# Feature matmuls on two halves of the array's rows, 65-column products on two halves of its columns

## The chip, the cores and the metric

One core of a Trainium2 chip runs the program. The metric is device time in microseconds (us). The kernel before takes 995.03 us, the median of three runs (994.74 to 995.92).

## The reference

Three layers run one after the other. The first is an attention without a softmax over the keys; the other two are feed-forward layers on 2304 tokens.

```python
# q, k, v: (4, 8, 576, 64) = batch, head, token, d;  omega: (128, 64)
def phi(x):                                   # x is scaled by 64 ** -0.25 first
    proj = einsum('bhsd,md->bhsm', x, omega)  # 128 features of each token
    h = proj - sum(x * x, -1, keepdims=True) / 2
    return exp(h - max(h, -1, keepdims=True)) / sqrt(128)
kv  = einsum('bhsm,bhsd->bhmd', phi(k), v)
z   = sum(phi(k), axis=2)
out = einsum('bhsm,bhmd->bhsd', phi(q), kv) / (einsum('bhsm,bhm->bhs', phi(q), z) + 1e-6)

x = out as (2304, 512)                        # d_ff 2048, then 1536
x = relu(x @ w_in) ** 2 @ w_out
x = rmsnorm(x) * g;  x = (silu(x @ w_gate) * (x @ w_val)) @ w_out2
```

Outside the kernel only the layout is changed. A column of ones stands beside v, so that one product of 65 columns gives both the numerator and the denominator.

## The kernel before, in words

Work goes by blocks: four of 512 tokens, one for each batch, and a remainder of 256 tokens (64 of each batch). Attention handles a batch as four pairs of heads. The 512 tokens of a pair are four tiles of 128 (`R` is 4), and the 64 left-over tokens of q and of k form one more tile for each pair, the remainder.

For one pair the PE does this. **Features** (L595 to L604): the transposed q or k of two heads stands as 128 rows (64 of d for one head, 64 for the other) by 512 tokens. Each tile of 128 tokens is the stationary operand, and the moving operand `bd` is block-diagonal, 128 rows by 256 columns, with omega for one head in the upper left and for the other in the lower right. So one matmul of depth 128 and 256 columns gives the features of both heads, and half of the products are with zeros. In batches 0 and 1 (`FULL` is 2) it is one plain fp32 matmul. In batches 2 and 3 operands are split into a high and a low part of type fp32r, and three fp32r matmuls stand for it; the split of each operand is a CAST on ACT and a subtraction on DVE or POOL (`operand`, L550). There are 36 tiles of features in a batch: four pairs by four of k, four of q and one of the remainder. **kv** (L671, L674): five matmuls of 65 columns for each head, four tiles and the remainder. **The output rows** (L731): four matmuls of 65 columns for each head. That makes 18 products of 65 columns in a pair and 72 in a batch, all plain fp32 with a stationary operand of 128 columns. Between them stand transposes through the array (L658, L726, L763, L773) and two 65-column products for the left-over queries (L735), whose stationary operand has 64 columns. A plain fp32 matmul stands in the trace as two records, each with its weight load.

DVE takes a maximum over each bank of features (L615) and two small operations (L619), and ACT the exponentials (L628). Further on the first feed-forward layer (`moe1`) has its hidden products at L845 and its output products at L875, all fp32r; the second layer has L1082 and L1143.

All instructions are nodes of a planner (`Plan`), which simulates the engines with the cost written beside each node and emits the nodes in the order in which its simulation starts them. Buffers come from classes with a fixed number of slots. PSUM has two banks of class `t`, two of `h`, four of `acc`. After batch 0 attention may use the two `t` banks alone. Until its own clock reaches 45 us, the planner also puts fillers on the PE where it finds nothing ready there: two fp32r matmuls of 256 columns on a constant (L484 to L487). An engine runs its instructions in the emitted order. All DMAs are issued from SP, in one order.

Attention of batch b+1 is planned beside `moe1` of batch b, and the weights of the second layer are brought into another form and stored to DRAM during the first.

Of the kernel before, what the change touches and what calls it, by code (L numbers as in the profile page):

```python
# [247 lines left out]
def kernel(  # L248
# [23 lines left out]
    nc = tc.nc  # L272
# [12 lines left out]
    FULL = 2  # L285
# [3 lines left out]
    EPS_DEN = 1e-6 * M  # L289

# [38 lines left out]
    plan.alloc["tr"] = slot_alloc("att", "tr", [P, 4, P], F32R)  # L329
    plan.alloc["tt"] = slot_alloc("att", "tt", [P, 4, P], F32R)  # L330
    plan.alloc["p"] = slot_alloc("att", "p", [P, 2 * R, M], F32)
    plan.alloc["pr"] = slot_alloc("att", "pr", [P, 2, M], F32)
# [16 lines left out]
    bd = const.tile([P, 2, M], F32, name="bd")  # L349
    bd_hi = const.tile([P, 2, M], F32R, name="bd_hi")  # L350
    bd_lo = const.tile([P, 2, M], F32R, name="bd_lo")
# [9 lines left out]
    b_bd, b_bds = Buf(ap=bd), Buf(ap=bd_hi)  # L361
# [14 lines left out]
    def dve(n):  # L376
        return 0.07 + n * 0.00104
# [87 lines left out]
    def emit_zero():  # L465
        nc.gpsimd.memset(bd, 0.0)

# [12 lines left out]
    plan.add("POOL", 0.5, T0, emit_zero, w=[b_bd])  # L480
# [14 lines left out]
    def emit_bd():  # L495
        for h in range(2):
            ps = slice(h * D, (h + 1) * D)
            nc.scalar.activation(out=bd[ps, h, :], in_=om2[ps, :], func=AF.Copy, scale=SCALE)

    def flat(t):  # L500
        return t.rearrange("p h m -> p (h m)")

    plan.add("ACT", 0.5, T0, emit_bd, [b_om, b_bd], [b_bd])
    split(T0 + (60 if FULL else 1), lambda: flat(bd), lambda: flat(bd_hi), lambda: flat(bd_lo), 256, [b_bd],
          (b_bds, 0), (b_bds, 1))

# [28 lines left out]
    def attention(b):  # L535
# [3 lines left out]
        full, long = b < FULL, b >= LONG  # L539
        rem_x = []  # L540
# [9 lines left out]
        def operand(prio, ldp, src, cls):  # L550

            if full:
                x = Buf(["lt", cls], view=lambda t: t if len(t.shape) == 2 else t.bitcast(F32).rearrange("p a n -> p (a n)"))
                dma(ldp, lambda: x.ap, src, 262144, w=[x])
                return x,
            x, th, tl = Buf(["lt"]), Buf([cls]), Buf([cls])
            dma(ldp, lambda: x.ap, src, 262144, w=[x])
            split(prio, lambda: x.ap, lambda: th.ap.rearrange("p a n -> p (a n)"),
                  lambda: tl.ap.rearrange("p a n -> p (a n)"), 512, [x], th, tl, "ANY")
            return th, tl  # L560
# [759 lines left out]
```

## Time and profile before

| | |
|---|---|
| median of three runs | 995.03 us |
| span of the profiled execution | 994.4 us |
| PE busy | 980.4 us, 99% |
| DVE, ACT, POOL busy | 72%, 53%, 10% |
| granted TensorE clock, mean | 1.000 |
| DMA, mean | 180 GB/s |

The page gives for the profiled execution its span, from the first to the last instruction; the median of the runs is 0.6 us above it, and this is taken as what lies around the span. A row of the timeline gives the start of a group of equal instructions, its length and its count. The end of a matmul is modelled and overlaps the next one, so the price of a record is read from the start of a group to the start of the next, divided by the count.

### The profile page before, as it was taken

Reading aid. Unit: us, or ns where it says so; the run is one execution under the profiler, and the core shown is the slowest. Engines: PE = TensorE matmul, PEld = TensorE weight load, DVE = VectorE, ACT = ScalarE, POOL = GpSimd, SP = SyncE. Lnnn points to the kernel's source line nnn. Section 1 sums busy time; section 2 is a strip of 40 time slices with the busy share of each in tenths; the row PEclk is TensorE's granted clock in tenths of the full one; section 3 lists DMA queues with packets and bytes.
Section 4 is the critical chain, followed back from the end, with each engine's and each line's share of the span. In section 5 each row is a group of like instructions: output and inputs, shape, how many; then the busy total and the mean of one; then the engine's idle time right before and its main releaser. Section 6 shows DMA issues by size and latency. Waiting matters only on the chain.

```text
span 994.4 us, 14580 instructions
## 1 busy us (share of the span) xinstructions
PE 980.4 (99%) x5130; PEld 832.7 (84%) x5130; DVE 712.0 (72%) x1393; ACT 523.7 (53%) x1093; POOL 100.5 (10%) x86
## 2 busy tenths in 40 slices
PE   8999999999999999999999999999999999999998
PEld 7878888888888888888789978888887888888887
DVE  6988998777658576665532989889798747576673
ACT  6988877665465455545444657664353444314220
POOL 2222222221110101000000101000000000000000
PEclk9999999999999999999999999999999999999999
DMA  8777888876667565778768534334234221212213
GB/s 270 240 245 259 278 287 292 300 267 214 248 217 257 189 248 188 237 247 285 273 222 273 169 107 150 93 117 127 77 116 136 75 64 53 74 43 75 65 32 105
DMA packets 74840, 179.35 MB, mean 180 GB/s; under 512 B 8848, under 2 KB 12048, under 8 KB 74768
## 3 DMA queue, kind: packets, MB, share of 16 engines
q1 hardware_dynamic: 74768, 178.43, 54.7%
q8 instruction: 40, 0.66, 0.3%
q14 instruction: 32, 0.26, 0.1%
HBM read 143.27 MB, written 35.13 MB: 179 GB/s over the span
## 4 chain that ended last, share of the span: by engine, by line
PE 86%; DVE 7%; DMA 3%; issue 1%; ACT 1%; SPq 0%; POOL 0%; ACTq 0%; DVEq 0%; POOLq 0%
PE acc L875 18%; PE h L845 18%; PE acc L1082 11%; PE t L1143 10%; PE h L1082 10%; PE t L1082 3%; PE t L731 3%; PE t L604 3%; PE t L671 2%; PE t L601 2%; DMA st<-y 2%; PE t L726 1%; DVE cc L1102 1%; PE h L1143 1%; DVE oa L1151 1%
## 5 line engine op out<-in xcount | busy, mean ns | idle before, releaser
L875 PE MATMUL acc<-g,wr 128*128 128x512 f32 (+1 forms) x660 | 151.9, 373 | 1.4 <-POOL g L394 1.2
L845 PE MATMUL h<-x,wr 128*128 128x512 f32 x528 | 133.9, 396 | 0.0
L875 PEld LDWEIGHTS acc<-g,wr 128*128 128x128 f32 x660 | 113.5, 189 | 21.5 <-POOL g L394 1.4
L1143 PE MATMUL t<-wq,ub 128*128 128x512 f32 x474 | 116.8, 391 | 1.5 <-DVE oa L1151 1.4
L403 ACT CAST wq<-wq 128x512 fp32r<-128x512 f32 x108 | 66.3, 619 | 98.1 <-DMA wq<-w2d3g 17.7
L845 PEld LDWEIGHTS h<-x,wr 128*128 128x128 f32 x528 | 97.2, 188 | 19.2
L1143 PEld LDWEIGHTS t<-wq,ub 128*128 128x128 f32 x474 | 88.4, 188 | 22.5 <-DVE oa L1151 2.9
L1082 PE MATMUL acc<-x,wq 128*128 128x512 f32 x324 | 106.9, 389 | 0.0
L394 DVE TENSOR_TENSOR wq<-wq 128x512 fp32r<-128x512 f32 x108 | 77.5, 726 | 29.5 <-ACT wq L403 29.2
L394 DVE TENSOR_TENSOR g<-f,g 128x512 fp32r<-128x512 f32 (+1 forms) x68 | 49.6, 729 | 65.9 <-ACT f L515 55.4
L859 ACT ACTIVATE f<-h 128x512 f32<-128x512 f32 (+1 forms) x80 | 45.1, 564 | 90.0 <-PE h L845 87.2
L1082 PE MATMUL h<-x,wq 128*128 128x512 f32 x252 | 85.3, 390 | 0.0
L1082 PEld LDWEIGHTS acc<-x,wq 128*128 128x128 f32 x324 | 60.8, 188 | 12.7
L875 PE MATMUL acc<-g,wu 128*128 128x512 f32 (+1 forms) x300 | 70.1, 375 | 1.2 <-DVE g L394 1.2
L1082 PE MATMUL acc<-xa,wq 128*128 128x512 f32 x192 | 69.8, 389 | 0.0
L628 ACT ACTIVATE p<-t,sm 128x128 f32<-128x128 f32 x212 | 59.2, 388 | 17.6 <-DVE sm L619 17.6
L1102 DVE TENSOR_TENSOR cc<-acc,cc 128x512 f32<-128x512 f32 x84 | 57.7, 687 | 13.6 <-PE acc L1082 11.8
L1151 DVE TENSOR_TENSOR oa<-t,oa 128x512 f32<-128x512 f32 x75 | 50.9, 687 | 21.8 <-PE t L1143 21.3
L845 PE MATMUL h<-x,wu 128*128 128x512 f32 x240 | 60.6, 395 | 0.0
L1082 PE MATMUL h<-xa,wq 128*128 128x512 f32 x168 | 60.5, 389 | 0.0
L875 PEld LDWEIGHTS acc<-g,wu 128*128 128x128 f32 x300 | 51.5, 189 | 10.5 <-DVE g L394 1.8
L441 ACT ACTIVATE dw<-st 128x512 f32<-128x512 f32 x67 | 45.6, 691 | 19.9 <-DMA st<-in_w_out_dram 8.1
(252 smaller groups left out, 1802.1 us busy)
## 6 DMA issues: line engine op xcount, KB each, us to landing
wr<-w1d SPq DMA_DIRECT2D x88, 512.0 KB, 4.3
st<-in_w_out_dram SPq DMA_DIRECT2D x28, 512.0 KB, 4.6
w1d<-wr SPq DMA_DIRECT2D x22, 512.0 KB, 4.6
st<-in_w_in_dram SPq DMA_DIRECT2D x16, 512.0 KB, 4.5
st<-in_w_gate_dram SPq DMA_DIRECT2D x12, 512.0 KB, 5.6
st<-in_w_val_dram SPq DMA_DIRECT2D x12, 512.0 KB, 5.4
st<-y SPq DMA_DIRECT2D x23, 256.0 KB, 4.2
v<-in_v_r_dram SPq DMA_DIRECT2D x16, 260.0 KB, 3.4
```

The source lines that it names most:

```text
L394: return lambda: en.tensor_tensor(out=lo(), in0=src(), in1=f32(hi()), op=ALU.subtract)
L403: first = plan.add("ACT", act(n), prio, lambda: nc.scalar.copy(out=hi(), in_=src()), rd, [whi], after, pre=[blo] if blo is not bhi else [])
L441: lambda: nc.scalar.activation(out=out(), in_=hf(), func=AF.Abs, scale=65536.0), [(st, 1)], [w])
L604: nc.tensor.matmul(o, lhsT=xs[x].ap[:, cidx, :], rhs=flat(w), start=n == 0, stop=n == 2)
L628: nc.scalar.activation(out=pbuf.ap[:, j0 + i, :], in_=fp.ap[:, i, :], func=AF.Exp, bias=mx.ap[:, i:i + 1])
L845: nc.tensor.matmul(hb.ap[:, :n], lhsT=u.ap[:, wl, kk * P:(kk + 1) * P], rhs=xcols(j, xl, kk)(), start=(gi == 0 and ii == 0), stop=(gi == l ...
L859: lambda: nc.scalar.activation(out=rb.ap[:, :n], in_=hb.ap[:, :n], func=AF.Relu), [hb], [rb])
L875: nc.tensor.matmul(accs[e].ap[:, :n], lhsT=u.ap[:, w, es], rhs=x.ap[:, :n], start=(c == 0 and i == 0), stop=(c == C1 - 1 and i == 2))
L1082: nc.tensor.matmul(bank.ap[:, cols], lhsT=u.ap[:, wl, c0 + kk * P:c0 + (kk + 1) * P], rhs=x[kk][xl].ap[:, :cols.stop - cols.start], start= ...
L1102: lambda: nc.vector.tensor_tensor(out=out.ap, in0=bank.ap, in1=x.ap, op=ALU.add), [bank, x], [out])
L1143: nc.tensor.matmul(o.ap, lhsT=x[xl].ap[:, c0:c0 + P], rhs=us[f"o{i}"].ap[:, wl, :], start=i == n == 0, stop=i == 1 and n == 2)
L1151: lambda: nc.vector.tensor_tensor(out=oa.ap, in0=o.ap, in1=oa.ap, op=ALU.add), [o, oa], [oa])
```

## The change

The block-diagonal operand goes. Its place takes `oms`, omega scaled, once on rows 0 to 63 and once on rows 64 to 127. Each tile of features becomes two plain fp32 matmuls of depth 64 and 128 columns: one head on the upper half of the array's rows, the other on the lower half, each into its own PSUM bank. This holds for all four batches, so the splits of batches 2 and 3 go, and the features of k (or of q) of a pair are always one node with two banks. The remainder is done once for a batch, for all four pairs at a time, with one buffer.

Each 65-column product becomes two, one for each half of the stationary operand's 128 columns; they write partitions 0 to 63 and 64 to 127 of the same bank. The costs that the planner is given for these nodes are changed with them, and some loads of the second layer wait for other nodes than before.

```diff
-    FULL = 2
+    HALVES = (slice(0, P // 2), slice(P // 2, P))
...
-    plan.alloc["pr"] = slot_alloc("att", "pr", [P, 2, M], F32)
+    plan.alloc["pr"] = slot_alloc("att", "pr", [P, 2 * HP, M], F32)
...
+    plan.add("ACT", 0.4, T0, lambda: nc.scalar.activation(out=oms, in_=om2, func=AF.Copy, scale=SCALE), [b_om], [b_oms])
...
-                            if full:
-                                nc.tensor.matmul(o, lhsT=xs[0].ap[:, c], rhs=flat(bd), start=True, stop=True)
-                                continue
-                            for n, (x, w) in enumerate(((0, bd_hi), (0, bd_lo), (1, bd_hi))):
-                                nc.tensor.matmul(o, lhsT=xs[x].ap[:, cidx, :], rhs=flat(w), start=n == 0, stop=n == 2)
...
+                fps = [Buf(banks, view=lambda t: t.rearrange("p (j m) -> p j m", m=M)) for _ in range(2)]
+                    for i in range(R):
+                        c = slice(i * P, (i + 1) * P)
+                        for h in range(2):
+                            ps = slice(h * D, (h + 1) * D)
+                            nc.tensor.matmul(fps[h].ap[:, i, :], lhsT=x.ap[ps, c], rhs=oms[ps, :], start=True, stop=True)
+                head = plan.add("PE", 0.24 * R + 0.2, p0, mm, [x, b_oms], fps, after, pre=[pbuf])
...
-            features(pb + 2 * u, pr, rem_x, [((hp,), 0, 2 * hp)], ssr)
+                rem_p[:] = [Buf(["pr"])]
+                features(pb + 2 * u, rem_p[0], rem_x[0], ODD, ssr)
...
                     for r in range(R):
-                        nc.tensor.matmul(
-                            kvp.ap[:, h, :D + 1], lhsT=pk.ap[:, h * R + r, :], rhs=vt[:, h, r, :], start=(r == 0), stop=False
-                        )
+                        for cs in HALVES:
+                            nc.tensor.matmul(kvp.ap[cs, h, :D + 1], lhsT=pk.ap[:, h * R + r, cs], rhs=vt[:, h, r, :],
+                                             start=(r == 0), stop=False)
...
                 for r in range(R):
-                    nc.tensor.matmul(np.ap[:, r * D1:(r + 1) * D1], lhsT=qt.ap[:, r * P:(r + 1) * P],
-                                     rhs=kvt[:, h, :], start=True, stop=True)
+                    for cs in HALVES:
+                        nc.tensor.matmul(np.ap[cs, r * D1:(r + 1) * D1],
+                                         lhsT=qt.ap[:, r * P + cs.start:r * P + cs.stop],
+                                         rhs=kvt[:, h, :], start=True, stop=True)
...
-    x01 = operands(0, rv01, E1 - 8.0, ["x", "xa"], [h3[9]], room)
+    x01 = operands(0, rv01, E1 - 8.0, ["x", "xa"], [h3[9], *last[-2:], *summed], room)
...
-    sets = [read_units(c, E1 + (c - 1.0 if c else -7.0), []) for c in range(NC2)]
+    sets = [read_units(c, E1 + (c - 1.0 if c else -7.0), held[:2]) for c in range(NC2)]
```

The order of the instructions moves in three places that matter here. The first is the PE in the first batch's attention, where `ones` marks a filler, `lt` and `tt` are transposed q or k, `p` the features after the exponential. Before:

```order
L486 MATMUL acc_182<-ones 128x256 x2
L601 MATMUL acc_278<-bd,tt_236 128x256 x2
L601 MATMUL t_293<-bd,tt_236 128x256 x2
L601 MATMUL t_307<-bd,lt_245 128x256 x2
L671 MATMUL h_314<-v_82,p_217 128x65 x4
L674 MATMUL h_314<-vr,pr_250 128x65
```

Now:

```order
L480 MATMUL acc_180<-ones 128x256 x4
L577 MATMUL t_289<-oms,lt_245 128x128
L577 MATMUL acc_290<-oms,lt_245 128x128
...
L480 MATMUL acc_180<-ones 128x256 x28
L577 MATMUL t_365<-oms,tt_249 128x128
L577 MATMUL acc_366<-oms,tt_249 128x128
...
L637 MATMUL acc_391<-v_80,p_213 64x65 x8
L640 MATMUL acc_391<-vr,pr_259 64x65 x2
```

A pair's features (four tiles, two matmuls each) now alternate between two banks, and fillers stand between them: 90 matmuls of fillers in all, where there were 16.

The second is the PE in the fourth batch's attention, among the first layer's products. Before, with `t` the bank of features or of kv:

```order
L845 MATMUL h_4018<-x_3676,wu_1085 128x512
L604 MATMUL t_4048<-bd_hi,tt_3723 128x256
L604 MATMUL t_4048<-bd_lo,tt_3723 128x256
L604 MATMUL t_4048<-bd_hi,tt_3724 128x256
...
L875 MATMUL acc_3809<-g_4148,wr_3824 128x512
L671 MATMUL t_4224<-v_83,p_4050 128x65 x4
L674 MATMUL t_4224<-vr,pr_4132 128x65
...
L658 MATMUL t_4224<-ident,pr_4132 128x64 x2
L875 MATMUL acc_3818<-g_4148,wr_3824 128x512
```

Now:

```order
L812 MATMUL h_4096<-x_3852,wr_3772 128x512
L577 MATMUL t_4107<-oms,tt_3038 128x128
L577 MATMUL t_4108<-oms,tt_3038 128x128
...
L812 MATMUL h_4096<-x_2896,wr_3772 128x512
...
L842 MATMUL acc_4013<-g_4101,wr_3814 128x512
L637 MATMUL t_4164<-v_80,p_3918 64x65 x8
L640 MATMUL t_4164<-vr,pr_4040 64x65 x2
...
L623 MATMUL t_4164<-ident,pr_4040 128x64 x2
L842 MATMUL acc_4021<-g_4101,wr_3814 128x512
```

Features and kv now stand between whole-array matmuls as groups on half arrays. Counted over the whole order, the PE changes between the whole array and a half (or from one kind of half to the other) 181 times, where it did 94 times: up to the last transposes of each batch 34, 54, 46 and 46 times, where it did 21, 24, 24 and 24 times.

The third is SP, where the blocks `y_87` and `y_88` are read back as the second layer's first operands. Before, where the same blocks are `y_89` and `y_90`:

```order
L388 DMA st_5573<-in_w_out_dram 128x1024
L388 DMA wr_5587<-w1d_94 128x1024
L388 DMA dw_5597<-y_90 128x512
L388 DMA wq_5607<-w2d0v_130 128x512
L388 DMA st_5620<-y_89 128x512
L388 DMA w2d5o_179<-dw_5604 128x512
```

Now:

```order
L386 DMA wr_6191<-w1d_111 128x1024
L386 DMA st_6211<-y_87 128x512
L386 DMA st_6221<-y_88 128x512
L386 DMA st_6233<-y_88 128x512
L386 DMA dw_6243<-y_87 128x512
L386 DMA wr_6254<-w1d_114 128x1024
```

The four loads now stand together, some ten rows further down, behind the last store of the rearranged weights.

## Rows read from the trace of the kernel before

**Rows 1.** The page, busy time of each engine, share of the span, instructions:

```profile
PE 980.4 (99%) x5130; PEld 832.7 (84%) x5130; DVE 712.0 (72%) x1393; ACT 523.7 (53%) x1093; POOL 100.5 (10%) x86
```

**Rows 2.** The PE's waits: engine, line, releaser, us in total, times, longest:

```profile
PE t L601 <- ACT p L628: 1.9, 2, 1.7
```

**Rows 3.** Stretches: length, then busy us of each engine, clock, DMA share, GB/s:

```profile
20.00:30.00 10.00, 10.00 (x82) 9.36 (x81) 8.71 (x33) 8.16 (x29) 1.04 (x1) 1.00 0.93 318
12.00:55.00 43.00, 42.56 (x295) 37.99 (x294) 37.27 (x122) 37.79 (x110) 12.29 (x10) 1.00 0.79 263
55.00:173.00 118.00, 116.05 (x612) 96.71 (x611) 107.21 (x248) 94.95 (x211) 29.02 (x21) 1.00 0.81 272
173.00:307.00 134.00, 134.00 (x747) 114.88 (x746) 94.71 (x217) 74.82 (x173) 22.79 (x19) 1.00 0.71 243
307.00:432.00 125.00, 125.00 (x706) 107.16 (x704) 81.89 (x201) 65.16 (x157) 12.52 (x10) 1.00 0.66 220
432.00:575.00 143.00, 140.45 (x795) 123.05 (x796) 74.45 (x118) 71.34 (x139) 8.00 (x8) 1.00 0.75 250
```

The columns after the length are PE, PEld, DVE, ACT and POOL.

**Rows 4.** Timeline of the PE, fp32 features: start us, length us, operation, count:

```profile
13.36 1.03 PE L601 MATMUL t<-bd,tt 128*128 128x256 f32 x4
14.22 1.03 PE L601 MATMUL t<-bd,lt 128*128 128x256 f32 x4
```

**Rows 5.** Timeline of the PE, twelve fp32r features, first and next:

```profile
226.91 0.28 PE L604 MATMUL t<-bd_hi,tt 128*128 128x256 f32 x1
...
228.30 1.07 PE L845 MATMUL h<-x,wr 128*128 128x512 f32 x4
```

**Rows 6.** Timeline of the PE, 65-column products, whole and 64 columns wide:

```profile
20.52 1.00 PE L731 MATMUL h<-kv,qt 128*128 128x65 f32 x8
21.45 0.45 PE L735 MATMUL h<-kv,qr 128*64 128x65 f32 x4
21.83 1.10 PE L731 MATMUL t<-kv,qt 128*128 128x65 f32 x8
22.77 1.06 PE L671 MATMUL acc<-v,p 128*128 128x65 f32 x8
23.66 0.39 PE L674 MATMUL acc<-vr,pr 128*128 128x65 f32 x2
```

**Rows 7.** Timeline of weight loads at L735, same stretch:

```profile
21.45 0.31 PEld L735 LDWEIGHTS h<-kv,qr 128*64 128x64 f32 x4
```

**Rows 8.** Weight loads grouped: busy us, mean ns of one, idle before:

```profile
L731 PEld LDWEIGHTS t<-kv,qt 128*128 128x128 f32 x240 | 30.7, 191 | 2.2
L735 PEld LDWEIGHTS t<-kv,qr 128*64 128x64 f32 x60 | 4.6, 136 | 1.0
```

**Rows 9.** Timeline of the PE, 128-column transposes:

```profile
25.92 0.60 PE L726 MATMUL h<-ident,p 128*128 128x128 f32 x4
26.35 0.60 PE L726 MATMUL acc<-ident,p 128*128 128x128 f32 x4
```

**Rows 10.** Timeline of the PE, one half-array transpose among whole-array work:

```profile
212.50 0.60 PE L773 MATMUL t<-ident,xw 128*128 128x128 f32 x4
213.03 0.27 PE L763 MATMUL t<-ident,xw 64*128 64x64 f32 x1
213.23 2.11 PE L845 MATMUL h<-x,wu 128*128 128x512 f32 x8
215.17 0.85 PE L875 MATMUL acc<-g,wr 128*128 128x512 f32 x3
```

**Rows 11.** Timeline of the PE, first layer's products alone:

```profile
461.50 2.88 PE L845 MATMUL h<-x,wr 128*128 128x512 f32 x12
464.22 2.88 PE L875 MATMUL acc<-g,wu 128*128 128x512 f32 x12
```

**Rows 12.** Splits of the transposed operands, grouped: busy us, mean ns, idle before:

```profile
L394 POOL TENSOR_TENSOR tt<-lt,tt 128x512 fp32r<-128x512 f32 x15 | 20.2, 1344 | 127.0 <-ACT tt L403 119.0 <-DMA st<-in_w_gate_dram 8.0
L403 ACT CAST tt<-lt 128x512 fp32r<-128x512 f32 x16 | 9.9, 621 | 17.2 <-PE t L604 9.2 <-issue 7.7
```

More of the change, by code (lines that the diff above doesn't have):

```diff
@@ L538, in attention @@
         lead = base - (6.0 if b else 2.85)
-        full, long = b < FULL, b >= LONG
-        rem_x = []
+        long = b >= LONG
+        rem_x, rem_p = [], []
         ssr = Buf(["sm"])
@@ L588, in transposed, with features @@
                 return xs
[L590 to L593 removed]
+            def features(p0, pbuf, x, places, ss, after=()):
+                fps = [Buf(banks, view=lambda t: t.rearrange("p (j m) -> p j m", m=M)) for _ in range(2)]
                 def mm():
[L596 to L622 removed]
@@ new lines, in mm, with mxop, less @@
+                    for i in range(R):
[4 more added lines that the diff above has]
+                head = plan.add("PE", 0.24 * R + 0.2, p0, mm, [x, b_oms], fps, after, pre=[pbuf])
+                for h, fp in enumerate(fps):
+                    mx = Buf(["sm"])
+                    p1 = p0 + 0.5 * u * h
+                    js = slice(*places[h])
+                    def mxop(fp=fp, mx=mx):
+                        nc.vector.tensor_reduce(out=mx.ap[:, :R], in_=fp.ap, op=ALU.max, axis=AX)
+                    def less(op, mx=mx, js=js):
+                        m = mx.ap[:, :R]
+                        nc.vector.scalar_tensor_tensor(out=m, in0=ss.ap[:, js], scalar=-SQH, in1=m, op0=ALU.mult, op1=op)
+                    plan.add("DVE", dve(M * R), p1, mxop, [fp], [mx])
@@ L629, in ex @@
                                                  bias=mx.ap[:, i:i + 1])
-                    plan.add("ACT", 0.25 * 2 * nr, p1, ex, [fp, mx], [(pbuf, j0)])
+                    plan.add("ACT", 0.25 * R, p1, ex, [fp, mx], [(pbuf, h)])
                 return head
-            def both(p0, pbuf, xs, ss, after=()):
-                g = [((0, 1), 0, 0), ((2, 3), 4, 4)]
-                if long:
-                    return features(p0, pbuf, xs, g, ss, after)
-                head = features(p0, pbuf, xs, g[:1], ss, after)
-                features(p0 + (0.5 if pbuf is pk else 1.0) * u, pbuf, xs, g[1:], ss)
-                return head
+            ODD = ((0, 2 * R, 2), (1, 2 * R, 2))
@@ L649, in pair @@
+            pr = rem_p[0]
             xq = transposed("q", pb + 2 * u)
-            last_q[:] = [both(pb + 4 * u, pq, xq, stats["q"])]
+            last_q[:] = [features(pb + 4 * u, pq, xq, ODD, stats["q"])]
             kvp = Buf(banks, view=lambda t: t[:, :2 * P].rearrange("p (h n) -> p h n", h=2))
@@ L985, in rms @@
             y = Buf(room if e else keep, view=fview)
-            dma(base, lambda y=y: y.ap[:, :n], lambda e=e: y_d[j][:, e, :], 512 * n, r=[(b_y[j], e), b_w2a], w=[y],
-                after=gates + used[-2:-1])
+            ld = dma(base, lambda y=y: y.ap[:, :n], lambda e=e: y_d[j][:, e, :], 512 * n, r=[(b_y[j], e), b_w2a], w=[y],
+                     after=gates + used[-2:-1])
+            if e == 0:
+                held.append(ld)
             nd = plan.add("ACT", act(n), base,
```

86 lines of the change are left out of this document (24 added, 62 removed), and 2 rows, old and new, of the table slots.

## The prediction

> **What bounds the kernel now.** I read the busy times first: the PE has work in 980.4 of 994.4 us, DVE in 712.0, ACT in 523.7 [rows 1]. The reader is to see that the PE alone has no slack over the whole. The waits of the PE come next. The longest of eight entries is 1.9 us [rows 2], so little is to be won by ending a wait, and the sum has to be made from the time that PE work takes. That holds only where nobody else is close behind, so the stretches come third [rows 3]. I cut them by batch: each batch's attention ends at its last transposes, near 55, 173, 307 and 432 us. In 173 to 432 us the PE is busy all the time and DVE in 94.71 of 134 and 81.89 of 125 us: time saved on the PE there is time saved. In 55 to 173 us DVE is busy in 107.21 of 118 us, and in 12 to 55 us DVE and ACT are at 37.27 and 37.79 of 43 us, with the DMA engines at 0.93 between 20 and 30 us: there a faster PE soon waits for the others. From 432 us on nothing on the PE is changed. Last I read the timeline for the prices.
>
> **Features.** A batch has 36 tiles of them. In batches 0 and 1 a tile is one plain fp32 matmul, two records of 256 columns. Four records take 14.22 - 13.36 = 0.86 us [rows 4], so a tile is 0.43 us and a batch 15.5 us. In batches 2 and 3 twelve fp32r matmuls take 228.30 - 226.91 = 1.39 us [rows 5], three to a tile: 0.348 us, a batch 12.5 us. Now a tile is four records, each of 128 columns and half the depth, two on each half of the rows. The nearest whole-array records of 128 columns, the transposes, come every (26.35 - 25.92) / 4 = 0.108 us [rows 9]; that is half of the 0.215 us of 256 columns. If the halves run side by side, a tile is 2 x 0.108 = 0.216 us and a batch 7.8 us. If they run one after the other with a weight load of 128 columns each, the price of a record is that of the 65-column ones, (23.66 - 22.77) / 8 = 0.111 us [rows 6], a tile 0.446 us, a batch 16.0 us.
>
> **65-column products.** A batch has 72, two records each: 72 x 2 x 0.111 = 16.0 us. These records last as long as 128-column ones although they move 65, and the same product with a stationary operand of 64 columns (L735) has its weight loads every (0.31 - 0.136) / 3 = 0.058 us [rows 7, 8]. So what is paid for here is the width of the weight load. Now a product is four records of that narrow shape: 2 x 0.058 = 0.116 us if the two column halves run side by side, a batch 8.4 us; 4 x 0.058 = 0.232 us if not, a batch 16.7 us.
>
> No row of before shows two halves at work at once; only one half is ever used. I take the lower price of both: the two halves have rows, columns and banks of their own, and the order alternates between them, so a load for the one has the other's matmul to hide behind.
>
> The pages of the Trainium skill differ on this. "TensorE: Matmul & The Clock Gate", section "LDWEIGHTS (loading the stationary operand)", says that a load costs by its columns and that fewer rows do not make it shorter. The trace agrees on the columns, 0.111 against 0.058 us; by that rule alone features gain nothing, and the sum would be the 994 us of the second rival below. "TensorEngine Tiling (Array Packing)", section "Key Properties", says that different tiles load and multiply in parallel; by that rule the sum is mine.
>
> **Changes between the whole array and a half.** The L735 group between two L731 groups takes, with the sixteen whole records about it, 22.77 - 20.52 = 2.25 us. Sixteen records at 0.111 and four at 0.058 are 2.01 us, so two changes cost 0.24 us [rows 6]. One half-array transpose among larger work: 215.17 - 212.50 = 2.67 us for five records at 0.108 and eight products of 512 columns at (464.22 - 461.50) / 12 = 0.227 us, 2.36 us; two changes cost 0.31 us [rows 10, 11]. So a change costs 0.12 to 0.16 us; I take 0.15, since most of the added ones stand among products of 512 columns. The order adds 13, 30, 22 and 22 of them in the four batches: 2.0, 4.5, 3.3 and 3.3 us.
>
> That a change of mode empties the array first is a rule of the Trainium skill too ("TensorEngine Tiling (Array Packing)", "Key Properties"). It speaks against this change, and the trace shows it with the 0.24 and 0.31 us above.
>
> **Fillers.** 74 matmuls of 256 fp32r columns more, at the 0.116 us of rows 5: 8.6 us, all in batch 0's stretch. They stand where the planner finds the PE idle, so they cost nothing if it is idle there and the whole 8.6 us if it is not.
>
> **What is hidden.** The splits of batches 2 and 3 go, 9.9 us on ACT and 20.2 us on POOL and little on DVE [rows 12]; these engines are not late there, so I credit nothing. The remainder of a batch is now done whole before its first kv, eight exponentials instead of two; in batch 0 this stands on the way, behind the fillers, in the others behind the first layer's products. The features now need both `t` banks at once in batch 1; if that stalls, it is part of what I take off there. The second layer's first operands are loaded later, behind the last weight store. The PE idles 2.55 us in all in 432 to 575 us [rows 3], and DVE is busy for half of that stretch and can take the operands later; I price it at nothing, between a gain of 2.5 us (all that idle time) and a loss of as much.
>
> **The sum.** If the PE alone decided, batch 0 would gain 15.5 + 16.0 - 7.8 - 8.4 - 2.0 - 8.6 = 4.7 us, batch 1 15.5 + 16.0 - 7.8 - 8.4 - 4.5 = 10.8 us, batches 2 and 3 12.5 + 16.0 - 7.8 - 8.4 - 3.3 = 9.0 us each. In batch 0 I take 2 us: DVE, ACT and DMA are near full. In batch 1 DVE has 118 - 107.21 = 10.8 us of free time at most, and cannot use all of it, since its work comes in chains with ACT; I take half, 5 us. The last two count in full. That is 25 us of the span, 994.4 - 25 = 969.4, and with the 0.6 us between span and median 970 us. Its own range is 960 us (the PE decides everywhere: 33.5 us) to 981 us (batches 0 and 1 give nothing, batches 2 and 3 14 us, with changes at 0.16 us and the halves some 0.02 us a tile or product slower than side by side).
>
> **Rivals.** First, the other engines take more. Batches 0 and 1 give nothing and half is lost in 2 and 3: 995 - 9 = 986 us. For it speaks DVE's 91% up to 173 us; against it that DVE has 39 and 43 us free in the next two stretches.
>
> Second, only one of the two kinds runs side by side. If the features do not, batch 0 gives 15.5 - 16.0 + 7.6 - 2.0 - 8.6 = -3.5 us, batch 1 -0.5 + 7.6 - 4.5 = 2.6, batches 2 and 3 -3.5 + 7.6 - 3.3 = 0.8 each: 994 us. If the 65-column products do not, -3.6, 2.5, 0.7 and 0.7 us: 995 us. For the former speaks that whole records already pay for their loads by the column; for the latter that starts would have to follow each other at 0.029 us, and the shortest spacing of records in the rows is 0.058.
>
> Third, slower: the halves run one after the other in both, each record waiting for the one before, at L577 and at L637 and L697. Features then lose 0.5 us a batch (3.5 in batches 2 and 3), products 0.7, changes and fillers cost their whole price: -11.8, -5.7, -7.5 and -7.5 us, 1027 us. It becomes slower than before as soon as the two kinds together save less than the 13.1 us of changes and the 8.6 us of fillers, that is less than about two fifths of the 55 us that side by side brings. For it speaks that no row shows two halves at once; against it that a load and a matmul of two records do overlap already (whole loads last 191 ns, products of 512 columns follow each other at 0.227 us [rows 8, 11]).
>
> **Chances.** My forecast 0.65; the other engines 0.09; one kind only 0.13; slower by serial halves 0.13. What can be told from no change is 0.2%, 2 us. The forecast and the first rival are faster; of the second, whose sum lies at the time of before, 0.04 is faster, 0.05 the same and 0.04 slower. So faster 0.78, same 0.05, slower 0.17. The range goes from 956 us (the fillers fall into idle time and halves overlap better than I priced) to 1000 us: it holds the forecast, the first and most of the second rival, and leaves the third out.
>
> **What would show it.** Records of one tile at L577 in pairs, eight groups of two records in about 0.9 us for four tiles; the ten 65-column products of a pair's kv in about 1.2 us, starts some 0.03 us apart on average. If records at L577 come every 0.11 us or those at L637 every 0.06 us, the halves run one after the other and the forecast is wrong. Weight loads should overlap in time between halves. Steps of 0.1 us or more should stand at each change. In 12 to 55 us the PE should stay near full through its fillers and DVE be near its limit; in 55 to 173 us the stretch should shorten by about half of the PE's saving. PE waits of more than 2 us on DVE or ACT before 173 us would show the first rival. If moe2 begins as late after the first layer's end as before, the moved loads cost nothing.

## The result and the profile after

The changed kernel takes 980.14 us, the median of four runs (978.55 to 983.48), where the kernel before took 995.29 in four runs of its own (994.74 to 995.92). The ratio is 0.985, with an interval of 0.9831 to 0.9869. So 15 us were gained where 25 were forecast: the forecast's side and its range hold, and ten of its microseconds are missing. The profiled execution took 981.26 us, with a span of 979.1 us and a mean granted clock of 0.995; before, the clock was 1.000. (Of the last kernel tried below, one run of four, at 1045.21 us and a granted clock of 0.848, is left out of the ratio.)

The busy times of the page, to set beside [rows 1]:

```profile
PE 960.5 (98%) x5996; PEld 794.5 (81%) x5996; DVE 690.7 (71%) x1363; ACT 513.9 (52%) x1075; POOL 73.8 (8%) x70
```

The PE has 20 us less work but only 15 us of them show: it now idles 18.6 us where it idled 14. The waits of the PE say where (engine, line, operation waited for, us in total, times, longest), to set beside [rows 2]:

```profile
PE h L812 <- ACT wu L401: 3.0, 1, 3.0
PE acc L842 <- POOL g L392: 2.1, 2, 1.2
PE t L577 <- ACT p L598: 1.4, 2, 1.2
PE t L1115 <- DVE oa L1123: 1.3, 5, 0.6
```

The longest is a new one: one of the first layer's products waits 3.0 us for a weight that ACT converts. The stretches, with the columns of [rows 3]:

```profile
12.00:55.00 43.00, 41.77 (x581) 36.44 (x578) 38.22 (x129) 36.29 (x110) 5.16 (x5) 0.99 0.83 272
55.00:173.00 118.00, 112.32 (x801) 86.09 (x802) 100.12 (x231) 89.21 (x192) 25.43 (x19) 0.96 0.79 260
173.00:307.00 134.00, 133.44 (x967) 107.00 (x965) 86.28 (x213) 75.98 (x176) 7.97 (x8) 1.00 0.79 261
307.00:432.00 125.00, 125.00 (x908) 100.59 (x907) 73.88 (x189) 63.68 (x155) 9.27 (x9) 1.00 0.65 220
432.00:575.00 143.00, 140.46 (x797) 123.08 (x796) 86.22 (x136) 77.48 (x147) 11.50 (x11) 1.00 0.75 253
```

From 173 us on the PE is still the bound, at full clock. From 55 to 173 us it is not: it is busy 112.32 us where it was 116.05, and the granted clock is 0.96 where it was 1.00. That is 3.7 us of idle time more and, at 0.04 of 118 us, 4.7 us of clock.

The timeline of the PE in the third batch's stretch gives the prices (start us, length us, line, operation, rows*columns of the weights, moving operand, count):

```profile
274.10 2.88 PE L842 MATMUL acc<-g,wr 128*128 128x512 f32 x12
276.91 1.16 PE L577 MATMUL t<-oms,tt 64*128 64x128 f32 x16
278.00 3.02 PE L812 MATMUL h<-x,wu 128*128 128x512 f32 x12
280.86 1.52 PE L842 MATMUL acc<-g,wr 128*128 128x512 f32 x6
282.31 0.69 PE L637 MATMUL t<-v,p 128*64 128x65 f32 x16
282.83 0.29 PE L640 MATMUL t<-vr,pr 128*64 128x65 f32 x4
282.94 0.64 PE L637 MATMUL t<-v,p 128*64 128x65 f32 x16
283.41 0.29 PE L640 MATMUL t<-vr,pr 128*64 128x65 f32 x4
283.63 0.34 PE L623 MATMUL t<-ident,pr 64*128 64x64 f32 x2
```

Four tiles of features, sixteen records, take 278.00 - 276.91 = 1.09 us. A record of L577 takes 0.272 us (the median of its group), so the last starts 1.16 - 0.27 = 0.89 us after the first. The first two of a group last 0.10 us longer than the others, so the other seven pairs take 0.79 us: 0.112 us a pair, 0.224 us a tile (forecast 0.216). The ten products of kv are forty records in 283.63 - 282.31 = 1.32 us. The first head's twenty take 282.94 - 282.31 = 0.63 us, 0.126 us a product with the entry into the group (forecast 0.116 without it).

The weight loads of the same stretch show the halves at work together (same columns):

```profile
276.91 0.97 PEld L577 LDWEIGHTS t<-oms,tt 64*128 64x128 f32 x16 [0.35 <-ACT g L828]
278.00 2.60 PEld L812 LDWEIGHTS h<-x,wu 128*128 128x128 f32 x12
```

Sixteen loads of the halves, 0.187 us each by the mean of their group, are 3.0 us of loading in 0.97 us: three are under way at a time. Twelve loads of the whole array, 0.189 us each, are 2.3 us in 2.60, one at a time; but these keep the pace of their 512-column products. Where the load set the pace before, at the 65-column products, loads of 0.191 us came every 0.111 us [rows 6, 8], fewer than two at a time.

Where the 15 us are is seen when each record of the PE is given the time to the start of the next one, over all records of both traces. What a change, a wait or a lower clock costs is then put on the record ahead of it.

| us of the PE | before | after | difference |
|---|---|---|---|
| 65-column products | 65.9 | 40.2 | -25.7 |
| features | 56.7 | 44.2 | -12.5 |
| left-over queries' products, transposes | 35.7 | 32.6 | -3.1 |
| fillers | 5.0 | 15.6 | +10.6 |
| first layer's products | 409.5 | 424.9 | +15.4 |
| second layer | 413.5 | 413.6 | +0.1 |

The first layer's products are the same in both kernels; they pay for the changes beside them, for the waits and for the clock. By time: where the same product of the first layer starts in both traces, with the same other work behind it (but for one tile of features at most), the kernel after is ahead by 3.3 us at 61 us of the time before, by 5.9 at 120, by 1.3 at 172, by 8.0 at 313, by 15.3 at 434, and by 15.3 at the end. (At the first such product, at 42 us, the starts do not compare: the kernel after has ten products of kv and two tiles of features more behind it.) So batch 0 gave 3.3 us, batch 1 gave 2.6 us and then lost 4.6, batches 2 and 3 gave 6.7 and 7.3, and the tail nothing.

Between the products at 61 and 172 us, over the same work, the two kernels read, before and then after:

```profile
60.91:171.59 110.68, 110.45 (x588) 92.30 (x586) 100.70 (x228) 89.06 (x195) 28.92 (x20) 1.00 0.81 272
57.57:170.25 112.68, 107.00 (x785) 82.18 (x783) 94.92 (x214) 84.78 (x185) 24.15 (x18) 0.97 0.79 257
```

After, the PE idles 5.7 us for 0.2, and at 0.03 of 112.68 us some 3.4 us go to the clock. Without these two it would have been 6.8 us shorter, and it was 2.0 us longer.

What was lost there stands in the timeline of the PE:

```profile
120.40 2.11 PE L812 MATMUL h<-x,wr 128*128 128x512 f32 x8
125.52 1.67 PE L812 MATMUL h<-x,wu 128*128 128x512 f32 x4 [3.01 <-ACT wu L401]
126.98 4.08 PE L842 MATMUL acc<-g,wr 128*128 128x512 f32 x12
```

and in four stretches of the second batch:

```profile
110.00:120.00 10.00, 10.00 (x96) 7.80 (x98) 10.00 (x24) 6.61 (x17) 0.00 (x0) 1.00 0.80 244
120.00:130.00 10.00, 6.99 (x31) 5.25 (x28) 7.02 (x18) 9.56 (x20) 2.26 (x2) 0.83 0.88 289
150.00:160.00 10.00, 8.19 (x54) 5.66 (x54) 6.25 (x15) 7.49 (x22) 2.86 (x3) 1.00 0.86 297
160.00:173.00 13.00, 13.00 (x113) 10.04 (x109) 11.41 (x28) 9.38 (x19) 2.21 (x2) 0.87 0.84 277
```

DVE is busy without a gap from 110 to 120 us, then ACT for 9.56 of 10 us, and the PE stands still for 3.01 us. Behind that the granted clock falls: four products take 126.98 - 125.52 = 1.46 us, 0.365 each where they take 0.227 at full clock [rows 11]. The last two rows show the same again, idle time ahead of 160 us and a granted clock of 0.87 behind it. Near 54 us, too, the clock fell after a wait of 1.16 us, and there three products took 56.29 - 54.84 = 1.45 us, 0.48 each, twice the price, that of the lower of the two clock levels (1.2 for 2.4 GHz):

```profile
53.55 1.36 PE L577 MATMUL t<-oms,tr 64*128 64x128 f32 x14 [1.16 <-ACT p L598]
54.84 1.65 PE L812 MATMUL h<-x,wr 128*128 128x512 f32 x3
56.29 1.48 PE L812 MATMUL h<-x,wu 128*128 128x512 f32 x3
```

### The profile page after: what moved, and what is told of

Its sections match the earlier page's. It is cut to its first block, busy times and chain, and to the rows that moved or that the text cites. A ratio compares the mean times of both kernels' runs of the same rounds, so it can differ in the third digit from the quotient of the medians.

```text
span 979.1 us, 16214 instructions
## 1 busy us (share of the span) xinstructions
PE 960.5 (98%) x5996; PEld 794.5 (81%) x5996; DVE 690.7 (71%) x1363; ACT 513.9 (52%) x1075; POOL 73.8 (8%) x70
## 4 chain that ended last, share of the span: by engine, by line
PE 84%; DVE 7%; DMA 5%; ACT 3%; issue 1%; SPq 0%; POOL 0%; DVEq 0%; ACTq 0%; POOLq 0%
PE h L812 18%; PE acc L842 17%; PE acc L1054 11%; PE t L1115 11%; PE h L1054 10%; PE t L1054 4%; PE t L577 3%; PE t L697 2%; PE t L637 1%; DVE cc L1074 1%; PE t L691 1%; PE acc L480 1%; PE h L1115 1%; DVE oa L1123 1%; DMA st<-in_w_out_dram 1%
## 5 line engine op out<-in xcount | busy, mean ns | idle before, releaser
L842 PE MATMUL acc<-g,wr 128*128 128x512 f32 (+1 forms) x660 | 154.4, 378 | 3.7 <-POOL g L392 2.1
L392 DVE TENSOR_TENSOR wq<-wq 128x512 fp32r<-128x512 f32 x108 | 80.1, 750 | 32.5 <-ACT wq L401 32.0
L392 DVE TENSOR_TENSOR g<-f,g 128x512 fp32r<-128x512 f32 (+1 forms) x64 | 43.3, 677 | 48.8 <-ACT f L499 36.8
L598 ACT ACTIVATE p<-t,sm 128x128 f32<-128x128 f32 x224 | 62.2, 383 | 16.4 <-DVE sm L590 16.1
L586 DVE TENSOR_REDUCE sm<-t 128x4 f32<-128x512 f32 x62 | 40.8, 684 | 28.3 <-PE t L577 26.7
```

The costliest lines, as they stand in the source:

```text
L392: return lambda: en.tensor_tensor(out=lo(), in0=src(), in1=f32(hi()), op=ALU.subtract)
L586: nc.vector.tensor_reduce(out=mx.ap[:, :R], in_=fp.ap, op=ALU.max, axis=AX)
L598: nc.scalar.activation(out=pbuf.ap[:, j, :], in_=fp.ap[:, i, :], func=AF.Exp, bias=mx.ap[:, i:i + 1])
L842: nc.tensor.matmul(accs[e].ap[:, :n], lhsT=u.ap[:, w, es], rhs=x.ap[:, :n], start=(c == 0 and i == 0), stop=(c == C1 - 1 and i == 2))
```

## The experiments

The theory after the result: the halves do run side by side; what is missing went to changes dearer than priced, to fillers that stand in the way, and in batch 1 to the preparation of weights on DVE and ACT, which a faster PE reaches too early. The rivals: one of the two kinds brings nothing, the moved loads of the second layer cost something, or the order of batch 1's attention is to blame and not the load of DVE. Each ratio below is to runs of the kernel before that were taken beside the experiment, with medians of 996.06 to 997.42 us, so that a time alone may differ from its ratio by 0.2%.

### One kind alone: e_rows, e_cols, and the waits alone: e_gates

e_rows is the kernel after with whole 65-column products.

```diff
-                        for cs in HALVES:
-                            nc.tensor.matmul(kvp.ap[cs, h, :D + 1], lhsT=pk.ap[:, h * R + r, cs], rhs=vt[:, h, r, :],
+                        nc.tensor.matmul(kvp.ap[:, h, :D + 1], lhsT=pk.ap[:, h * R + r, :], rhs=vt[:, h, r, :],
...
-                    for cs in HALVES:
-                        nc.tensor.matmul(np.ap[cs, r * D1:(r + 1) * D1],
+                    nc.tensor.matmul(np.ap[:, r * D1:(r + 1) * D1], lhsT=qt.ap[:, r * P:(r + 1) * P],
```

> Features on two halves of the rows as in the changed kernel, the 65-column products whole as before. Theory: the halves run side by side, a tile of features costs 0.224 us against 0.43 (batches 0, 1) and 0.348 us (2, 3), that is 23.7 us less; 66 more changes between whole and half array at 0.2 us give back 13 us and 38 more filler matmuls up to 4 us; batch 1 wins nothing because weight preparation on ACT and DVE is late there. 989 to 993 us. Rival (changes cost nothing beyond what their rows show at entry, 0.1 us, and the loss in batch 1 comes from the 65-column products): 981 to 985 us.

It took 988.41 us, a ratio of 0.9925 (0.99 to 0.9949): 7.5 us gained, a little more than the theory's. No wait of the PE is longer than 1.3 us and the clock is 1.0.

e_cols is the kernel before with the 65-column products on halves and the changed waits of the second layer's loads.

```diff
-                        nc.tensor.matmul(
-                            kvp.ap[:, h, :D + 1], lhsT=pk.ap[:, h * R + r, :], rhs=vt[:, h, r, :], start=(r == 0), stop=False
-                        )
+                        for cs in HALVES:
+                            nc.tensor.matmul(kvp.ap[cs, h, :D + 1], lhsT=pk.ap[:, h * R + r, cs], rhs=vt[:, h, r, :],
+                                             start=(r == 0), stop=False)
...
-                    plan.add("PE", 0.224 * 5, pb + 3 * u + h * u, kv, [(pk, h * R), pr, bv, b_vr, b_vz], [(kvp, h)],
+                    plan.add("PE", 0.13 * 5, pb + 3 * u + h * u, kv, [(pk, h * R), pr, bv, b_vr, b_vz], [(kvp, h)],
```

> The 65-column products on two halves of the columns as in the changed kernel, features as before (one matmul of depth 128, splits in batches 2 and 3), and the changed waits of the second layer's loads. Theory: 288 products at 0.117 instead of 0.223 us are 30.5 us less, 33 more changes at 0.2 us give back 6.6, 22 more filler matmuls up to 2.6, batch 1 wins little: 978 to 983 us, so this part alone is worth as much as both. Rival (both parts count as the sum of the changed kernel divides them by their rows, two thirds to one third): 985 us.

It took 987.69 us, a ratio of 0.9915 (0.9892 to 0.9937): 8.5 us, less than the theory's, and near the rival's. Its trace shows why. At 288 us it is 10 us ahead of the kernel before, and then the PE waits for ACT in one place. The timeline of its PE:

```profile
306.51 0.98 PE L776 MATMUL t<-ident,xw 128*128 128x128 f32 x4 [3.25 <-ACT p L629]
...
311.06 0.79 PE L848 MATMUL h<-x,wr 128*128 128x512 f32 x1 [1.57 <-ACT x L404]
...
314.00 3.36 PE L848 MATMUL h<-x,wr 128*128 128x512 f32 x8
317.20 1.08 PE L848 MATMUL h<-x,wu 128*128 128x512 f32 x4
```

and its stretches there:

```profile
300.00:310.00 10.00, 5.31 (x23) 3.20 (x21) 5.29 (x17) 3.64 (x11) 1.26 (x1) 0.83 0.86 287
310.00:320.00 10.00, 8.94 (x33) 7.30 (x34) 6.65 (x17) 4.85 (x11) 0.73 (x1) 0.65 0.42 147
```

A wait of 3.25 us is followed by a granted clock of 0.83 and 0.65, a second wait, and products at (317.20 - 314.00) / 8 = 0.40 us. There it loses 13 us and falls 3 us behind the kernel before; the last batch brings it to 7 ahead in these two executions. So the miss is not in the price of the products. The two kinds' gains apart, 7.5 and 8.5 us, make about the 15 us of both, but that is luck: e_cols lost 13 us in a place of its own, the kernel after lost some 9 us of idle time and clock in batch 1, and e_rows has neither loss.

e_gates is the kernel before with only the changed waits.

```diff
-    x01 = operands(0, rv01, E1 - 8.0, ["x", "xa"], [h3[9]], room)
+    x01 = operands(0, rv01, E1 - 8.0, ["x", "xa"], [h3[9], *last[-2:], *summed], room)
...
-    sets = [read_units(c, E1 + (c - 1.0 if c else -7.0), []) for c in range(NC2)]
+    sets = [read_units(c, E1 + (c - 1.0 if c else -7.0), held[:2]) for c in range(NC2)]
```

> The kernel before with only the changed waits of the second layer's loads (first operands behind the last weight store and the sums, unit reads behind the first loads of the sums). Theory: these loads are early enough either way, 994 to 997 us. Rival: they give or cost some of the difference, 2 us or more either way.

It took 995.21 us, where the kernel before took 997.42 beside it, a ratio of 0.998 (0.9968 to 0.9993). In the kernel before, the moved loads are worth about 2 us of gain (0.7 to 3.2), at the edge of the 2.5 us to either side that the forecast left them.

### Serial halves: e_serial

The same records, but in each node all of one half first.

```diff
-                    for i in range(R):
-                        c = slice(i * P, (i + 1) * P)
-                        for h in range(2):
+                    for h in range(2):
+                        for i in range(R):
+                            c = slice(i * P, (i + 1) * P)
...
-                    for r in range(R):
-                        for cs in HALVES:
+                    for cs in HALVES:
+                        for r in range(R):
```

> The changed kernel's nodes in the changed kernel's order, but within a node all matmuls of one half come first and then all of the other, so that no two neighbours are on different halves (but at one place in a node). Theory: the gain comes from halves running side by side; now a tile of features is 0.446 instead of 0.224 us and a product 0.232 instead of 0.117 us, together 65 us more on the PE, of which a few hide in batch 0 and 1: 1030 to 1045 us. Rival (the smaller shapes themselves are cheaper, neighbours don't matter): 980 us.

It took 1009.95 us, a ratio of 1.0144 (1.0111 to 1.0178): 30 us more than the kernel after, with the same number of records. So the gain hangs on the alternation of the halves, and the rival that the order does not matter is refuted. By the account over all records, features rise from 44.2 to 61.2 us and the 65-column products from 40.2 to 57.9. But it is less than the theory expected, and the timeline of its PE tells why:

```profile
208.65 1.71 PE L577 MATMUL t<-oms,tt 64*128 64x128 f32 x16
210.29 3.03 PE L841 MATMUL acc<-g,wu 128*128 128x512 f32 x12
...
215.06 0.74 PE L637 MATMUL t<-v,p 128*64 128x65 f32 x10
215.58 0.22 PE L639 MATMUL t<-vr,pr 128*64 128x65 f32 x1
215.64 0.22 PE L637 MATMUL t<-v,p 128*64 128x65 f32 x1
215.64 0.22 PE L639 MATMUL t<-vr,pr 128*64 128x65 f32 x1
```

Four tiles of features take 1.64 us, 0.55 us more than after: 0.224 + 0.55 / 4 = 0.36 us a tile, where one half strictly behind the other would be 0.446. And at L637 eight records of the first half are written ahead of its two of L639; in the trace ten start ahead of the first of L639. Two of them belong to the second half, which has begun while the first is not done.

### The fillers: e_fill12

```diff
-    FILL = (0.6, 45.0, 0.21)
+    FILL = (0.6, 12.0, 0.21)
```

> The changed kernel with the fillers allowed until 12 us of the planner's clock instead of 45: 28 filler matmuls instead of 90. Theory: the fillers stand in time in which the PE would wait anyhow, so 978 to 982 us. Rival (the PE bounds batch 0 and the fillers cost their whole price): 62 matmuls at 0.116 us less, 973 us. Third possibility: without them the granted clock falls in more stretches, 983 us or more.

It took 975.71 us, a ratio of 0.9796 (0.9769 to 0.9822): 4.5 to 5.5 us less than after, for 62 matmuls fewer (28 for 90), which at 0.116 us are 7.2 us. This lies between the theory and the rival, but the stretches show that neither names the place of the gain. The kernel after:

```profile
30.00:40.00 10.00, 10.00 (x159) 9.21 (x157) 8.83 (x33) 9.16 (x27) 2.04 (x2) 1.00 0.82 249
40.00:50.00 10.00, 10.00 (x129) 8.49 (x126) 8.83 (x29) 7.66 (x20) 0.00 (x0) 1.00 0.79 260
```

e_fill12:

```profile
30.00:40.00 10.00, 8.54 (x128) 6.90 (x128) 8.27 (x30) 10.00 (x30) 1.42 (x2) 1.00 0.62 206
40.00:50.00 10.00, 7.73 (x71) 5.89 (x68) 9.02 (x24) 5.33 (x15) 2.14 (x2) 1.00 0.91 284
50.00:60.00 10.00, 7.39 (x34) 5.48 (x35) 9.16 (x18) 6.75 (x15) 4.13 (x3) 0.83 0.53 188
```

Without the fillers the PE idles 3.7 us between 30 and 50 us, with ACT busy for all of 30 to 40 us and DVE for 17.3 of the 20. Behind that comes the longest of its waits, near 51 us, and the third possibility, a lower clock (0.83):

```profile
PE h L812 <- ACT x L401: 3.1, 1, 3.1
```

By the starts of the same products e_fill12 is 4.0 us ahead of the kernel after at 49 us of that kernel's time, 0.4 at 58, 1.7 behind at 118, 3.1 ahead at 131 and 4.5 at 419. So in these two executions nothing of the gain is left at the end of batch 0. It comes at 125 us, where e_fill12, whose order in batch 1 is another, has no wait for `wu`. What a filler costs by itself is not shown.

### The load of DVE: e_light_after, e_light_before

Both leave one DVE instruction out of each of the 68 units of weights that are rebuilt (L441, 0.487 us in the mean, 33.1 us in all).

```diff
-        plan.add("DVE", Shared(0.345), prio,
-                 lambda: nc.vector.tensor_scalar(out=out(), in0=out(), scalar1=EXP_LO, scalar2=EXP_HI, op0=ALU.max,
-                                                 op1=ALU.min), [w], [w])
```

> The changed kernel without the clamp in the decoding of the weights (one DVE operation of 128x512 for each of 68 units, some 0.4 us each; part of the decoding is left out). Theory: in batch 1 the PE waits for weights that DVE and ACT prepare, and falls to the lower clock after it; with 10 us less DVE work between 55 and 173 us these waits go: 970 to 974 us. Rival (the stall comes from the order of the nodes or from PSUM banks): 978 to 980 us.

It took 968.74 us, a ratio of 0.971 (0.9687 to 0.9733).

> The kernel before without the same clamp (part of the decoding is left out). Theory: there the PE bounds this stretch and DVE's relief hides: 992 to 995 us, so that the distance to the changed kernel with the same edit grows from 15 to about 21 us. Rival: both kernels gain the same, the distance stays at 15 us.

It took 995.69 us, a ratio of 0.9985 (0.9974 to 0.9997). The kernel before gains next to nothing by a lighter DVE, the kernel after 11 to 14 us. With the lighter DVE the distance of the two is 27 us (0.971 / 0.9985 = 0.9725), somewhat more than the 25 us forecast. In the stretch of batch 1, e_light_after:

```profile
55.00:173.00 118.00, 116.38 (x871) 91.33 (x873) 105.36 (x221) 90.07 (x209) 31.70 (x23) 1.00 0.85 289
```

The PE is busy 116.38 us at a granted clock of 1.00 and starts 871 records there, 70 more than after. DVE is even busier than after, since it gets on faster: a share near nine tenths was not what told that it held the PE up, the wait of 3.0 us was, and it is gone (the longest left is 1.4 us, for a DMA). By the starts of the same products batch 1 now gives 9.4 us: e_light_after is ahead of the kernel before by 3.9 us at 61 us and by 13.3 at 169. But the planner knows of the lighter DVE, so the order in batch 1 is another one too, and the load of DVE is not tested apart from the order.

### The order of batch 1: e_long1

`LONG` is the first batch in whose attention kv of both heads and the transposes of the left-over queries are one node, and the output rows of both heads another; below it they are nodes of their own.

```diff
-    LONG = 2
+    LONG = 1
```

> The changed kernel with batch 1 planned in the joined nodes of batches 2 and 3 (LONG is 1), fillers to 45 us. Ten changes fewer are 2 us; the longer nodes hold the PE for longer at a time. Theory (batch 1 is short of prepared weights, not of order): 977 to 980 us. Rival (the order of batch 1 makes the waits): 970 to 975 us.

It took 974.14 us, a ratio of 0.9772 (0.9755 to 0.9789): 6 to 8 us less than after for ten changes fewer (171 for 181). That is more than the changes can be worth, and it is the rival's number. In its stretch of batch 1:

```profile
55.00:173.00 118.00, 115.08 (x847) 91.39 (x848) 110.72 (x251) 91.82 (x200) 21.88 (x16) 0.99 0.83 276
```

The PE has 2.8 us less of idle time there, the clock is 0.99 for 0.96, and it has no wait for `wu`. By the starts of the same products it is 1.3 us behind the kernel after at 114 us and 7.0 ahead at 170 us. So another order cures batch 1's loss with the same instructions on DVE. That DVE's little room is a second condition is argued and not shown, since e_light_after changes the order with the load; nor is it shown that the work behind the waiting product was ready.

### The changes: e_wholetr

The transposes of the left-over queries go through the whole array instead of half of its rows, and 64 of the 128 columns that come out are copied.

```diff
-                    nc.tensor.transpose(o[:, h, :], pr.ap[:SR, h0 + h, :], ident[:SR, :SR])
+                    nc.tensor.transpose(o[:, h, :], pr.ap[:, h0 + h, :], ident)
```

> The changed kernel with one edit: the two transposes of a pair's left-over queries read all 128 rows of the remainder's features instead of 64, so they need no mode of their own. Changes between whole and half array fall from 181 to 162, the transposes themselves keep their price. Theory: 19 changes at 0.2 us are 3.8 us, 975 to 978 us. Rival (a change costs 0.1 us, as the step at its entry): 978 to 980 us.

It took 977.84 us, a ratio of 0.9815 (0.98 to 0.983), that is 0.0035 less than after: 3.5 us for 19 changes fewer (162 for 181), 0.18 us each. The intervals of the two ratios all but touch, so this alone is weak, and the trace does not bear the division out. By the starts of the same products e_wholetr is ahead of the kernel after by 0.1 us at 118 us and by 2.4 at 166: its wait for `wu` is 2.5 us for 3.0, and the clock does not fall again near 160 us. In batches 2 and 3, where 8 changes fewer stand alone, it gains 1.0 us, 0.13 each, and the rest behind 419 us. That 0.18 is near the price by the timeline, below, is luck.

### Together: b_flw, b_lw45, b_lw30

All three have `LONG = 1` and the whole transposes, with 157 changes in b_flw, and fillers until 12, 45 and 30 us.

```diff
-    FILL = (0.6, 45.0, 0.21)
+    FILL = (0.6, 30.0, 0.21)
-    LONG = 2
+    LONG = 1
-                    nc.tensor.transpose(o[:, h, :], pr.ap[:SR, h0 + h, :], ident[:SR, :SR])
+                    nc.tensor.transpose(o[:, h, :], pr.ap[:, h0 + h, :], ident)
```

> The changed kernel with three edits that take work from the PE: fillers until 12 instead of 45 us of the planner's clock, batch 1 planned with the joined nodes of batches 2 and 3 (LONG is 1), and the two transposes of the left-over queries on the whole array (128 rows) instead of 64 rows. Changes between whole and half array fall from 181 to 157. Theory (a change costs 0.2 us on the PE): 24 changes less are 4.8 us, fillers 4 us as measured apart, so 969 to 972 us. Rival (changes cost little, 0.1 us, or the time goes into waits of batch 1 again): 973 to 977 us.

It took 967.95 us, a ratio of 0.9713 (0.968 to 0.9747).

> The best version so far with its fillers allowed until 45 us again (90 filler matmuls for 28); joined nodes in batch 1 and whole-array transposes stay. Theory: 62 fillers cost some 4 us as in the pair measured before, 970 to 973 us. Rival (they keep the clock up, which fell for 10 us near 51 us in the best version): 963 to 967 us.

It took 972.64 us, a ratio of 0.976 (0.9745 to 0.9774). The difference to b_flw is 4.7 us, as between e_fill12 and the kernel after, but it is not the price of the fillers from 12 us on: by the starts of the same products b_flw is 3.3 us ahead at 49 us, 0.4 behind at 58, 0.5 ahead at 414 and 4.9 at 516.

> The best version so far with fillers until 30 us of the planner's clock, 56 filler matmuls. Theory: between the two, 968 to 971 us. Rival (fillers where the PE waits cost nothing and keep the clock up, later ones cost): 963 to 967 us.

It took 966.1 us, the median of three (963.01 to 967.19), a ratio of 0.9703 (0.9684 to 0.9722). By the intervals it is no better than b_flw. It beats both kernels: 29 us under the one before and 14 under the one after. Its stretches of the first two batches:

```profile
12.00:55.00 43.00, 39.68 (x554) 33.51 (x551) 39.72 (x130) 38.12 (x115) 6.48 (x6) 1.00 0.83 273
55.00:173.00 118.00, 116.54 (x867) 93.37 (x866) 106.02 (x246) 97.01 (x209) 22.42 (x17) 1.00 0.87 293
```

The clock is 1.00 and no single wait of the PE is longer than 1.2 us (the traced execution is the fastest of the three, 963.01 us). It is 5.5 us ahead of b_flw at 69 us of that kernel's time, with 28 fillers more: b_flw waits 3.0 us for `x` near 51 us, and its clock is 0.70 in 55 to 65 us. With the same DVE instructions as after, batch 1 runs as it did with the lighter DVE, 116.54 us and 867 records against 116.38 and 871.

## Why the prediction was right, and what it mis-sized

**The halves run side by side: right, and nearly at the price forecast.** A tile is 0.224 us (0.216 forecast). The ground given holds for features alone: the halves of a 65-column product have columns of their own but the same rows and the same bank, and run side by side all the same. The rule that a load costs by its columns whatever its rows holds for one load, 0.187 us for 64 rows against 0.189 for 128, but it did not decide: two loads for different halves run at once. So the second rival, built on it, is out, and e_serial shows what the alternation is worth, 30 us. (The rule is that of the Trainium skill, "TensorE: Matmul & The Clock Gate", "LDWEIGHTS (loading the stationary operand)"; the trace agrees with it on the single load, and with "TensorEngine Tiling (Array Packing)", "Key Properties", on the pair.)

**A change: 0.2 us, not 0.15.** In the third batch a group of features among products costs more than its 1.09 us: the twelve products ahead take 276.91 - 274.10 = 2.81 us, 0.09 over 12 x 0.227, and the twelve behind 280.86 - 278.00 = 2.86, 0.14 over. That is 1.32 us in all; over the 18 such groups of batches 2 and 3 the median is 1.31. Eight pairs at 0.112 are 0.90, so its two changes cost 0.42 us, 0.21 each. For changes beside a pair's left-over transposes e_wholetr gives 0.13 in the same batches. The forecast read the price from four records of L735 and one transpose, and took the dearer of the two, 0.16, as the bound; groups of sixteen records cost more than either. Over the 87 added changes, 0.05 us more are 4.4 us. The group before took 1.39 us [rows 5]: in batches 2 and 3, then, features on halves gain 0.07 us a group, nearly nothing, and nearly all that these batches gained is the 65-column products' (25.7 / 4 = 6.4 us a batch). In kv the ten products went from 2.2 us, by the price of [rows 6], to 1.32.

**Batches 2 and 3: right within the prices.** 9.0 us each were forecast; with 22 changes at 0.2 it is 7.9, the tiles and products, dearer by 0.008 and up to 0.010 us, take at most 1.0 us more, and 6.7 and 7.3 were measured.

**Batch 1: the term that was mis-sized.** Half of 10.8 us was taken, on the ground that DVE had 10.8 us free and works in chains with ACT; measured are 2.0 us of loss. By 120 us batch 1 had given 2.6. Then one wait of 3.0 us for a converted weight, the lower clock behind it and another fall of the clock near 160 us took 4.6. What no step had is that such a wait is paid again in clock: over the same work, 5.5 us of idle time more and 3.4 us of clock, against 6.8 us that the PE's own work fell by (10.8 - 30 x 0.05 = 9.3 with the changes at 0.2).

The forecast's first rival named this mechanism with the right stretch, and its sign in the profile, a wait of more than 2 us on DVE or ACT before 173 us, did come. Batches 0 and 1 gave 1.3 us together, where the rival had nothing and the forecast 7; batches 2 and 3 gave 14.0, where the rival had 9 and the forecast 18. So 980 us lies nearer to the rival's 986 than to the forecast's 970, and a range of 956 to 1000 us tells little between the two.

**Batch 0: 3.3 us, where 2 were taken.** The fillers were priced at 8.6 us if they stand in the way and nothing if not. No run shows their price: without 62 of them the PE came 4.0 us earlier to 49 us, and a wait with a lower clock behind it took 3.6 of that again (e_fill12).

**The hidden parts: right.** The splits of POOL and ACT are gone (POOL 100.5 to 73.8 us), and in 173 to 432 us the PE is busy 258.4 of 259 us without them. The moved loads gain about 2 us in the kernel before (e_gates), where they were priced at nothing, but from 434 us on both kernels run alike: the idle time of the PE in 432 to 575 us is 2.54 us where it was 2.55 [rows 3].

**The missing ten, by batch.** 7.0 us in batch 1 and 4.0 in batches 2 and 3, of which 2.2 are the changes, less 1.3 that batch 0 gave more. With another order, fewer fillers and 29 changes fewer (152), b_lw30 gains 29 us, beside the 33.5 that the forecast had for a PE that decides everywhere.

## What to carry to other kernels

Products of few columns that pay for their weight loads run nearly twice as fast on alternating halves of the array, rows or columns; but each change between whole and half costs about 0.2 us, so that work on halves has to be put together in groups, and a group of 1 us gains next to nothing against a form that is not much dearer. Fillers meant for idle time cannot be priced by their count where the order is fixed ahead: with fewer of them the PE came earlier to its next wait, and the order behind it was another. And when the engine that bounds gets faster, look in the stretch where a helper is above nine tenths for the first thing that is made late for it: the waits there cost more than half as much again in clock, and another order cured it with the same instructions on that helper.

## What the runs showed that was not expected

In the trace the PE does not keep the program's order between the halves: in e_serial records of the second half start while two of the first are still to come, and features cost 0.36 us a tile instead of 0.446. The Trainium skill ("TensorE: Matmul & The Clock Gate", "Part 3: Packing small matmuls — row/col tiling") has matmuls start strictly in the order of the program; the starts in this trace do not agree, and the measurement decides.

The clock fell after short waits: after one of 1.16 us, 3 products of 512 columns took 0.48 us each, and after one of 3.25 us in e_cols the granted clock was 0.83 and then 0.65 in stretches of 10 us. Before the change the PE had waits as long as 1.7 us [rows 2] and a mean clock of 1.000; what tells the one case from the other was not settled here.
